# First MLP in eight blocks of 504 positions, the second weight's products interleaved with k's

## The chip, the cores and the metric

The kernel runs on one core of one Trainium2 chip. Its time is the device time of one execution in microseconds; three runs of the kernel before took 1005.41, 1000.34 and 1002.55, median 1002.55. TensorE (PE, with its weight loads PEld), VectorE (DVE), ScalarE (ACT), GpSimd (POOL) and SyncE (SP, which issues the DMAs) run their own instruction lists side by side and wait for each other on semaphores.

## What is computed

Eight batches of 576 positions, 512 features. An attention over 32 memory slots gives x, a first MLP (token shift, squared ReLU, sigmoid gate) gives x2, a second MLP (spatial gate) gives the output:

```python
# attention, per batch and head
a = softmax(phi, axis=positions); k_m = a.T @ k; v_m = a.T @ v
x = softmax(q @ k_m.T / sqrt(64)) @ v_m
# first MLP
x_prev = concatenate([zeros, x[:, :-1]])
xk = mu_k * x + (1 - mu_k) * x_prev
xr = mu_r * x + (1 - mu_r) * x_prev
k = maximum(xk @ w_k, 0.0)                 # 512 -> 1024
v = k * k @ w_v                            # 1024 -> 512
x2 = v / (1.0 + exp(-(xr @ w_r)))          # 512 -> 512
# second MLP
h = maximum(x2 @ w_in, 0.0); u, v = halves(h)
v_s = w_spatial @ layer_norm(v) + b_spatial
out = (u * v_s) @ w_out
```

## The kernel before

Features lie on the partitions, positions in the columns. Every fp32 factor is held as a high and a low part, and a product is three matmuls: high by high, low weight by high, high weight by low (`three`). `split` makes the two parts: a copy on ACT (high, L123) and a subtraction on DVE (low, L124). Weights come in as 64-bit floats, and `load_f64` turns each stretch into fp32 and splits it (ACT L161 and L177, DVE L169, L171 and L178).

The first MLP runs over sixteen half batches of 288 positions (HB). Half batch i has three phases. `k_phase` makes eight products of 12 matmuls (four chunks of features times three) in banks 0 to 3 by turns; each goes through Relu (ACT L725) and, two at a time, Square (L727) and a split into kh and kl (L123, L124). `r_phase` makes four products of 12 matmuls, each with a Sigmoid (L743) into r. `v_product` makes four products of 24 matmuls over the eight chunks of kh and kl, multiplies by r on DVE (L764) and stores x2 to DRAM. That is 240 matmuls of 288 columns. `prep_x` makes the operands xk and xr of the next half batch, 288 columns at a time: two scaled copies of x and x shifted (ACT L432, DVE L436) and a split.

Between the products `pump()` runs the generator `att` one step further, which writes the attention of later batches (`att_step`, two for each batch) into the same instruction lists; its small products use banks 4 to 7. The attention of the first batch (its two steps 0 and 1) is written at the start together with w_k. Step 1 works in borrowed room: its scores lie in the tile `r`, its operands in `kh`, `W3h` and `W3l`. w_v comes in later, into `W3h` and `W3l`, once step 1 is done with them.

Tiles are named by tags with one buffer each: a new tile of a tag waits until the last one has had its last reader. So `tile_of("r", ...)` in `r_phase` waits for step 1 of the attention, and the Relus of the first `k_phase` do not, since they write the tiles `t0` and `t1`. A scheduler orders the list of each engine; PE, ACT and DVE then run their lists in order.

From half batch 13 on, `w_in_steps` brings in and splits w_in. In the last half batch `load_x2(0)` splits the x2 of batch 0 for the second MLP (`uv(0)`), whose first half is written between the last half batch's v products.

Of the kernel before, what the change touches and what calls it, by code (L numbers as in the profile page):

```python
# [27 lines left out]
HALF = 256  # L28
KC = DM // 128
# [17 lines left out]
def kernel(  # L47
# [200 lines left out]
    def att_step(i):  # L248
# [5 lines left out]
        n_small = (3, 0)[i] if i < 2 else 5  # L254
# [77 lines left out]
        for halves in ((0,), (1,)) if i < 2 else ((0, 1),):  # L332
# [3 lines left out]
            scs = {hf: bank(4 + hf)[:, 0:HB] for hf in halves}  # L336
# [48 lines left out]
            if g == 0 and halves[0] == 0:  # L385
                xT[b] = tile_of(f"xT{b % 2}", [128, KC, S + 1])
                nc.gpsimd.memset(xT[b][:, :, 0:1], 0.0)
            for pr in range(2):
# [12 lines left out]
                if i >= 2:  # L401
                    yield True
# [11 lines left out]

    def pump():
        n = slot[0]
        slot[0] += 1
        for _ in range(0 if n < 14 else 3 if n < 28 else 1):
            next(att, None)
        next(more[0], None)  # L420
# [3 lines left out]
    x32_tags = turns("x32a", "x32b")  # L424
    mm = turns(0, 1, 2, 3)

    def prep_x(i, which, c):
        b, hf = divmod(i, 2)
        x32 = tile_of(next(x32_tags), [128, HB])
        n = which * KC + c  # L430

        nc.scalar.activation(  # L432
            out=x32, in_=xT[b][:, c, hf * HB:(hf + 1) * HB], func=ACTF.Copy,
            scale=mu_sb[:, 2 * KC + n:2 * KC + n + 1],
        )
        nc.vector.scalar_tensor_tensor(  # L436
            out=x32, in0=xT[b][:, c, 1 + hf * HB:1 + (hf + 1) * HB], scalar=mu_sb[:, n:n + 1], in1=x32,
            op0=ALU.mult, op1=ALU.add,
        )

        both = operand((n + KC) % (2 * KC) if i == 2 * B - 1 else n)[:, 0:2 * HB]
        h, lo = both[:, 0:HB], both[:, HB:]
        split(x32, h, lo)
        xs[i, which, c] = (h, lo)
# [12 lines left out]
            tile_of("W3h", [128, 4096]), q1, tile_of("r", [128, 2 * S]), tile_of("o0", [128, HB]),  # L457
            tile_of("o1", [128, HB]), tile_of("W3l", [128, n_r], F32R),
# [29 lines left out]
    for c in ORDER:  # L488
# [5 lines left out]
        elif c == "x":  # L494
            prep_x(0, 0, next(xk_chunks))
# [27 lines left out]
    def early(n):  # L523

        for c in FIRST_BLOCK[n]:
            if c == "r":
                next(w_r_steps)
            elif c == "v":
                next(w_v_steps)
            elif c == "n":  # L530
                with tc.issue_after(fetches[-1].ins):
                    load_step(2)
            elif c == "x":
                prep_x(0, 1, next(xr_chunks))
            else:
                stage(first[c == "b"])
# [4 lines left out]
    def w_in_steps():  # L541
# [64 lines left out]
        while not w2_free:  # L606
            yield
        parts_of("W1", wi_u)
        for _ in range(3):
            yield  # L610
        for q, a in ((0, a11), (1, a12), (4, s2), (3, s1), (5, a21), (6, s4), (2, a22)):
            split(a, wi_u[0][:, q], wi_u[1][:, q])
# [3 lines left out]
    last = 2 * B - 1  # L616
    w2_free, xT_free, att_free, late_free, xs_free = [], [], [], [], []
    copied, added, tails, left_v, normal = [None], [None], {}, [], []

    def load_x2(n):  # L620
# [6 lines left out]

        def fetch_x2(dst, k, half):
            sl = slice(half * HALF, (half + 1) * HALF)
            if rest and half == 1:  # L630

                sl = slice(HALF, 2 * HALF - 64)
                for c in range(2):
                    tails[2 * k + c] = dst[:, c, HALF - 64:]
                dst = dst[:, :, 0:HALF - 64]
            src = x2r.rearrange("p c b s -> p c (b s)") if rest else x2d[n]
            nc.sync.dma_start(out=dst, in_=src[:, 2 * k:2 * k + 2, sl])
# [16 lines left out]
        def put(q, x):  # L654
            ts[q] = place(q)

            with behind(*([copied[0]] if rest or (n == 0 and xs_free) else normal if n > 1 else ())):
                split(x, *ts[q])

        if rest:  # L660
# [17 lines left out]
            while not late_free:  # L678
                yield
            yield  # L680
# [4 lines left out]
        else:  # L685
# [14 lines left out]
            while not xs_free:  # L700
                yield
# [11 lines left out]
    def k_phase(i, after=lambda m: None):  # L713
        xk = [xs.pop((i, 0, c)) for c in range(KC)]
        kh, kl = pair("k", [128, FC, HB])
        for m in range(FC):
# [6 lines left out]
            if m % 2 == 0:  # L723
                ks = tile_of(f"t{m // 2 % 2}", [128, 2 * HB])
            nc.scalar.activation(out=ks[:, m % 2 * HB:(m % 2 + 1) * HB], in_=acc, func=ACTF.Relu)  # L725
            if m % 2 == 1:
                nc.scalar.activation(out=ks, in_=ks, func=ACTF.Square)  # L727
                ks = ks.rearrange("p (c s) -> p c s", c=2)
                copied[0] = split(ks, kh[:, m - 1:m + 1, :], kl[:, m - 1:m + 1, :])
            after(m)  # L730
        return kh, kl

    def r_phase(i, after):
        xr = [xs.pop((i, 1, c)) for c in range(KC)]
        r = tile_of("r", [128, KC, HB])
# [9 lines left out]
        return r  # L745

    def v_product(i, m, kh, kl, r, between=lambda: None):
        b, hf = divmod(i, 2)
# [565 lines left out]
```

## Time and profile before

| | |
|---|---|
| median of the runs | 1002.55 us |
| profiled execution | 1001.31 us, of it span 999.5 us |
| PE busy | 976.6 us, 98% of the span |
| DVE, ACT, POOL busy | 704.2, 632.5, 94.7 us |
| mean granted TensorE clock | 0.998 |
| matmuls in the program: 288, 256, 512 columns | 4872, 1596, 336 |

The timeline gives each row's start and length in us; rows of equal instructions are merged, with their number behind x. Busy times of matmuls overlap, so what a matmul costs in a stream is read from the distance between starts. The half batches run from 39 us to some 615 us; w_v is awaited until 79 us; the second MLP takes the rest.

### The profile page before, as it was taken

The page shows a single profiled execution, that of the slowest core. Times are in us where ns is not written, and L with a number is a line of the kernel's source. Part 1 is how long each engine was busy: PE and PEld are TensorE (multiplying, and loading weights), DVE is VectorE, ACT ScalarE, POOL GpSimd, SP SyncE. Part 2 cuts the span into 40 slices and gives each one's busy share as a digit, 9 for nine tenths or more (in the row PEclk, how much of TensorE's full clock was granted, in tenths as well). Part 3 has the DMA queues.
Part 4 walks back from the last instruction along what each step waited for, and adds up shares of the span by engine and source line. Part 5 has one row for each costly group of instructions (what it writes and reads, how often), then busy time and mean ns, then how long its engine had stood idle before and what let it go on. Part 6 is the DMA issues. An engine that isn't in the chain of part 4 may idle for free.

```text
span 999.5 us, 19803 instructions
## 1 busy us (share of the span) xinstructions
PE 976.6 (98%) x7844; PEld 935.6 (94%) x7844; DVE 704.2 (70%) x1477; ACT 632.5 (63%) x1285; POOL 94.7 (9%) x70
## 2 busy tenths in 40 slices
PE   6889999999999999999999999999999999999998
PEld 5778999999999999999999999999999999998787
DVE  4989965665675576567569537768777767779983
ACT  4897884676687667568557647836554644564653
POOL 0000000000000000000013020022012402203320
PEclk9999999999999999999999999999999999999999
DMA  9587422332233323421032142231142223155633
GB/s 285 160 261 243 153 87 68 105 109 98 60 103 115 104 60 93 126 91 31 19 120 82 50 118 68 81 112 37 56 132 90 76 80 90 58 181 168 209 146 116
DMA packets 84300, 110.86 MB, mean 111 GB/s; under 512 B 15984, under 2 KB 67568, under 8 KB 81904
## 3 DMA queue, kind: packets, MB, share of 16 engines
q1 hardware_dynamic: 84208, 109.60, 34.7%
q8 instruction: 61, 1.00, 0.4%
q14 instruction: 31, 0.25, 0.1%
HBM read 79.30 MB, written 30.28 MB: 110 GB/s over the span
## 4 chain that ended last, share of the span: by engine, by line
PE 82%; ACT 6%; DVE 6%; DMA 4%; issue 1%; SPq 0%; POOL 0%; DVEq 0%; ACTq 0%; POOLq 0%
PE bank L104 79%; PE bank L287 2%; DMA st<-in_w_in 2%; DMA st<-in_w_v 1%; DMA ATh<-in_kv 1%; PE bank L339 1%; ACT xT L398 1%; ACT kh L123 1%; DVE xs L124 1%; ACT t L727 1%; ACT t L725 0%; ACT xs L123 0%; ACT x32a L432 0%; DMA st<-in_w_r 0%; ACT st L161 0%
## 5 line engine op out<-in xcount | busy, mean ns | idle before, releaser
L104 PE MATMUL bank<-xs,W1h 128*128 128x288 f32 (+1 forms) x1496 | 246.7, 292 | 2.2 <-DVE o L764 1.2
L104 PEld LDWEIGHTS bank<-xs,W1h 128*128 128x128 f32 x1496 | 211.3, 188 | 7.4 <-issue 5.8
L104 PE MATMUL bank<-xs,W1l 128*128 128x288 f32 (+1 forms) x748 | 135.4, 290 | 0.0
L104 PEld LDWEIGHTS bank<-xs,W1l 128*128 128x128 f32 x748 | 110.6, 188 | 0.2 <-issue 0.2
L104 PE MATMUL bank<-kh,W3h 128*128 128x288 f32 x576 | 98.7, 297 | 2.6 <-ACT W3h L177 2.1
L104 PE MATMUL bank<-xs,W2h 128*128 128x288 f32 (+2 forms) x572 | 97.2, 305 | 1.2 <-ACT xs L123 0.6
L124 DVE TENSOR_TENSOR kl<-t,kh 128x576 fp32r<-128x576 f32 x64 | 49.5, 774 | 59.8 <-ACT kh L123 59.3
L104 PE MATMUL bank<-kh,W3l 128*128 128x288 f32 x544 | 90.0, 296 | 0.0
L104 PEld LDWEIGHTS bank<-xs,W2h 128*128 128x128 f32 x572 | 83.1, 188 | 6.6 <-issue 2.5
L104 PEld LDWEIGHTS bank<-kh,W3h 128*128 128x128 f32 x576 | 83.4, 188 | 5.1 <-ACT W3h L177 3.0
L725 ACT ACTIVATE t<-bank 128x288 f32<-128x288 f32 x128 | 50.9, 402 | 56.9 <-PE bank L104 56.5
L104 PE MATMUL bank<-kl,W3h 128*128 128x288 f32 x544 | 86.1, 296 | 0.0
L104 PEld LDWEIGHTS bank<-kh,W3l 128*128 128x128 f32 x544 | 77.9, 188 | 0.8 <-issue 0.7
L104 PEld LDWEIGHTS bank<-kl,W3h 128*128 128x128 f32 x544 | 77.0, 188 | 0.0
L104 PE MATMUL bank<-ATh,xs 128*128 128x256 f32 x472 | 73.5, 278 | 0.0
L124 DVE TENSOR_TENSOR xs<-st,xs 128x512 fp32r<-128x512 f32 (+1 forms) x60 | 53.4, 904 | 17.2 <-ACT xs L123 17.1
L104 PEld LDWEIGHTS bank<-ATh,xs 128*128 128x128 f32 x472 | 63.2, 188 | 0.0
L123 ACT ACTIVATE xs<-st 128x512 fp32r<-128x512 f32 (+1 forms) x60 | 35.8, 623 | 39.5 <-POOL st L650 35.7
L650 POOL TENSOR_TENSOR st<-st 128x512 f32<-128x512 f32 x16 | 23.5, 1467 | 247.2 <-DVE xs L124 246.5
L104 PE MATMUL bank<-ATl,xs 128*128 128x256 f32 x236 | 46.3, 278 | 0.0
L727 ACT ACTIVATE t<-t 128x576 f32<-128x576 f32 x64 | 43.7, 683 | 1.3
L104 PE MATMUL bank<-xs,W2l 128*128 128x288 f32 x256 | 44.2, 295 | 0.0
(291 smaller groups left out, 2015.2 us busy)
## 6 DMA issues: line engine op xcount, KB each, us to landing
ATh<-in_kv SPq DMA_DIRECT2D x14, 1300.0 KB, 6.6
ATl<-in_qT SPq DMA_DIRECT2D x30, 288.0 KB, 4.4
st<-x2d SPq DMA_DIRECT2D x32, 256.0 KB, 3.9
ATh<-in_phin SPq DMA_DIRECT2D x15, 320.0 KB, 3.1
x2d<-o SPq DMA_DIRECT2D x32, 144.0 KB, 2.0
st<-in_w_in SPq DMA_DIRECT2D x8, 512.0 KB, 4.1
ATh<-gd SPq DMA_DIRECT2D x8, 512.0 KB, 5.2
out_T<-W3h SPq DMA_DIRECT2D x16, 256.0 KB, 2.2
```

What stands on the lines that cost most here:

```text
L104: x = nc.tensor.matmul(out=out, lhsT=pairs[i][0], rhs=pairs[i][1], start=fresh and i == 0, stop=i == n - 1, skip_group_check=not fresh,)
L123: high = nc.scalar.activation(out=h, in_=x, func=ACTF.Copy)
L124: low = nc.vector.tensor_tensor(out=lo, in0=x, in1=h.bitcast(F32), op=ALU.subtract)
L287: x = nc.tensor.matmul(out=kvp[32 * j:32 * j + 32, :], lhsT=ph[0:n, t, 32 * j:32 * j + 32], rhs=kv[0:n, t, j, :], start=(t == 0), stop=(t ...
L339: x = nc.tensor.matmul(out=scs[hf][32 * j:32 * j + 32, :], lhsT=kmT[64 * hf:64 * hf + 64, 32 * j:32 * j + 32], rhs=q[64 * hf:64 * hf + 64, ...
L398: nc.scalar.activation(out=xT[b][:, 2 * g + pr, 1 + hf * HB:1 + (hf + 1) * HB], in_=xo, func=ACTF.Copy)
L650: engine.tensor_tensor(out=out, in0=a, in1=b, op=ALU.subtract)
L725: nc.scalar.activation(out=ks[:, m % 2 * HB:(m % 2 + 1) * HB], in_=acc, func=ACTF.Relu)
L727: nc.scalar.activation(out=ks, in_=ks, func=ACTF.Square)
```

## The change

Half batches 0 and 1 stay as they are in form. The other seven batches (4032 positions) become eight blocks of 504 positions that run across the batches' borders. A block has the same 240 matmuls, with 504 columns each. The order of its products is K0 K1 K2 V0 K3 V1 ... K7 V5 R0 R1 R2 V6 R3 V7: `V(c)` adds the products of chunk c of k to all four v accumulators at once (banks 0 to 3, three matmuls each), so only three chunks of k are kept at a time, in a ring cut from kh and kl (a fourth part holds the last chunk of xr). K and R use banks 4 and 5; the attention keeps banks 6 and 7. `prep_x` works on stretches that end at batch borders and calls the attention on where its x isn't written yet. In `k_phase` the Relus now write into the back of the tile `r`, and r itself is its front. `pump()` runs 0.95 attention steps a call in the blocks. x2 overwrites r and is stored from there. `uv(0)` starts after the last block, v and u mixed, and `load_x2(B)`, which brings the batches' last 64 positions, is called inside it.

```diff
+WB = 504
+NB = (T - S) // WB
...
-        n_small = (3, 0)[i] if i < 2 else 5
+        n_small = (3, 0)[i] if i < 2 else 6
...
-            scs = {hf: bank(4 + hf)[:, 0:HB] for hf in halves}
+            scs = {hf: bank((4 if wide else 6) + hf)[:, 0:HB] for hf in halves}
...
+                while b > 2 and b - 2 not in mixed:
+                    yield True
                 xT[b] = tile_of(f"xT{b % 2}", [128, KC, S + 1])
...
+        while p < p1:
+            b, s0 = divmod(p, S)
+            while b > 0 and G * b + c // G not in written:
+                next(att)
+            w = min(p1 - p, S - s0)
...
-        while not w2_free:
+        while not w1_free:
...
         kh, kl = pair("k", [128, FC, HB])
+        room = tile_of("r", [128, 6, HB])
+        r, ks = room[:, 0:KC], room[:, KC:]
...
-            if m % 2 == 0:
-                ks = tile_of(f"t{m // 2 % 2}", [128, 2 * HB])
-            nc.scalar.activation(out=ks[:, m % 2 * HB:(m % 2 + 1) * HB], in_=acc, func=ACTF.Relu)
+            nc.scalar.activation(out=ks[:, m % 2, :], in_=acc, func=ACTF.Relu)
...
+        x2 = r[:, m, :]
+        nc.vector.tensor_tensor(out=x2, in0=acc, in1=x2, op=ALU.mult)
+        store_x2(m, x2, HB * i, HB * i + HB)
...
-    for i in range(last):
+    for i in range(2):
...
+    pace[:] = 0.0, 0.95
+    rings = [tile_of(tag, [128, 4, WB], F32R) for tag in ("kh", "kl")]
+    slots = [rings[0][:, 0:2], rings[0][:, 2:4], rings[1][:, 0:2]]
+    last_xr = rings[1][:, 2:4].rearrange("p a s -> p (a s)")
+    k_banks = turns(4, 5)
...
+        def K(m):
+            acc = wide_product(wk, m, 0, pump)
+            h, lo = (slots[m % 3][:, n] for n in range(2))
+            x = tile_of("t2", [128, WB])
+            nc.scalar.activation(out=x, in_=acc, func=ACTF.Relu)
+            nc.scalar.activation(out=x, in_=x, func=ACTF.Square)
+            copied[0] = split(x, h, lo)
...
+        def V(c):
+            if c == 0:
+                v_accs.extend(bank(n)[:, 0:WB] for n in range(KC))
+            h, lo = (slots[c % 3][:, n] for n in range(2))
+            for m in range(KC):
+                ms = slice(m * 128, (m + 1) * 128)
+                pairs = (wv[0][:, c, ms], h), (wv[1][:, c, ms], h), (wv[0][:, c, ms], lo)
+                for n, (a, b) in enumerate(pairs):
+                    nc.tensor.matmul(
+                        out=v_accs[m], lhsT=a, rhs=b, start=c == 0 and n == 0,
+                        stop=c == FC - 1 and n == 2,
+                    )
...
+        order = [(K, 0), (K, 1)]
+        for c in range(FC - 2):
+            order += [(K, c + 2), (V, c)]
+        order += [(R, 0), (R, 1), (R, 2), (V, 6), (R, 3), (V, 7)]
+        for n, (f, c) in enumerate(order):
+            f(c)
+            if f is K and c < KC:
+                prep_x(1, c, p0, p1, last_xr if c == KC - 1 else None)
...
+            if n in (13, 14, 15, 16) and j < NB - 1:
+                prep_x(0, n - 13, p1, p1 + WB)
...
+        for m in range(KC):
+            x2 = r_all[0][:, m, :]
+            added[0] = nc.vector.tensor_tensor(out=x2, in0=v_accs[m], in1=x2, op=ALU.mult)
+            store_x2(m, x2, p0, p1)
...
+    for n, item in enumerate(uv(0).items()):
+        item()
+        if n in (2, 12, 14, 16, 18, 23, 25):
+            next(x2_steps)
```

Three places of the instruction lists. ACT in the first half batch, before: t_388 is the Relus' tile, L161 and L177 turn w_r.

```order
L161 ACTIVATE xT_403<-xT_403 128x1024
L432 ACTIVATE x32a<-xT_271,mu 128x288
L725 ACTIVATE t_388<-bank_375 128x288
L432 ACTIVATE x32b<-xT_271,mu 128x288
L725 ACTIVATE t_388<-bank_441 128x288
L727 ACTIVATE t_388<-t_388 128x576
```

ACT now, from the same part of the list on (asp and W3l are the split scores of attention steps 0 and 1, L402 the attention's result, L732 the Relu):

```order
L125 ACTIVATE asp<-ATl 128x288
L163 ACTIVATE xT_576<-xT_576 128x1024
L125 ACTIVATE W3l<-r 128x288
L125 ACTIVATE xs_513<-t_510 128x288
L402 ACTIVATE xT_269<-bank_516 128x288
L402 ACTIVATE xT_269<-bank_521 128x288
L732 ACTIVATE r<-bank_374 128x288
L732 ACTIVATE r<-bank_439 128x288
```

The first two Relus moved behind the split of step 1's scores, which lie in r.

PE in a later half batch, before, where the r products end and the v products begin (rows of the attention between left out):

```order
L104 MATMUL bank_2154<-xs_1898,W2h 128x288
...
L104 MATMUL bank_2185<-kh,W3h 128x288 x8
L104 MATMUL bank_2185<-kh,W3l 128x288 x8
L104 MATMUL bank_2185<-kl,W3h 128x288 x8
L104 MATMUL bank_2229<-kh,W3h 128x288 x8
```

PE now, from the end of K2 through V0 (kh and its neighbour are the ring) to K3:

```order
L106 MATMUL bank_4228<-xs_4063,W1h 128x504
L847 MATMUL bank_4254<-kh,W3h 128x504
L847 MATMUL bank_4254<-kh,W3l 128x504
L847 MATMUL bank_4254<-kh,W3h 128x504
L847 MATMUL bank_4255<-kh,W3h 128x504
...
L847 MATMUL bank_4257<-kh,W3h 128x504
L106 MATMUL bank_4274<-xs_3970,W1h 128x504
```

A v product no longer runs through all chunks in one bank; three matmuls of one chunk go to each of four banks between two products of k.

DVE now, at the border of two blocks (L882 is x2, L454 prep_x, L349 and L358 attention, the last row the low part of K0):

```order
L882 TENSOR_TENSOR r<-bank_3703,r 128x504
L126 TENSOR_TENSOR xs_4225<-t_4220,xs_4225 128x504
L454 SCALAR_TENSOR_TENSOR t_4246<-xT_3196,mu,t_4246 128x360
L454 SCALAR_TENSOR_TENSOR t_4246<-xT_3750,mu,t_4246 128x144
L454 SCALAR_TENSOR_TENSOR t_4297<-xT_3196,mu,t_4297 128x360
L454 SCALAR_TENSOR_TENSOR t_4297<-xT_3750,mu,t_4297 128x144
L126 TENSOR_TENSOR xs_4251<-t_4246,xs_4251 128x504
L349 STREAM_TRANSPOSE ATl<-bank_4182 128x288
L349 STREAM_TRANSPOSE ATl<-bank_4183 128x288
L126 TENSOR_TENSOR kl<-t_4297,kl 128x504
L358 TENSOR_REDUCE ATl<-ATl 128x18
L126 TENSOR_TENSOR kh<-t_4169,kh 128x504
```

Before, x2 was made product by product between prep_x's instructions; now four of 504 columns stand together there, ahead of the low part that V0 reads.

## Rows read from the trace of the kernel before

**Rows 1.** Windows: stretch, length, busy us of each engine (instructions), granted clock, DMA share, GB/s.

```profile
core 0: us, PE busy (x) PEld busy (x) DVE busy (x) ACT busy (x) POOL busy (x), PEclk, DMA share, GB/s
12.00:16.00 4.00, 3.53 (x45) 2.78 (x46) 1.04 (x5) 0.00 (x0) 0.00 (x0) 0.59 1.06 364
...
36.00:60.00 24.00, 21.83 (x156) 20.36 (x156) 23.56 (x50) 22.93 (x50) 0.00 (x0) 1.00 0.53 169
60.00:80.00 20.00, 16.49 (x148) 15.12 (x147) 16.83 (x31) 17.28 (x31) 0.33 (x1) 1.00 0.95 287
...
200.00:480.00 280.00, 279.54 (x2456) 271.14 (x2455) 176.64 (x386) 193.47 (x397) 0.42 (x4) 1.00 0.28 89
600.00:640.00 40.00, 40.00 (x332) 39.87 (x331) 31.44 (x76) 29.54 (x69) 0.00 (x0) 1.00 0.26 80
```

**Rows 2.** Timeline of PE, 288 columns: start, length, engine, line, operands, count.

```profile
317.75 0.69 PE L104 MATMUL bank<-xs,W2l 128*128 128x288 f32 x4
...
322.51 0.69 PE L104 MATMUL bank<-xs,W2l 128*128 128x288 f32 x4
...
323.57 1.22 PE L104 MATMUL bank<-kh,W3h 128*128 128x288 f32 x8
...
329.96 0.70 PE L104 MATMUL bank<-asp 128*128 128x288 f32 x4
```

**Rows 3.** Timeline of PE, 256 columns (second MLP) and 512 columns (last products).

```profile
621.76 0.39 PE L104 MATMUL bank<-xs,W1l 128*128 128x256 f32 x2
...
624.57 0.40 PE L104 MATMUL bank<-xs,W1l 128*128 128x256 f32 x2
...
951.10 0.63 PE L104 MATMUL bank<-W1l,kh 128*128 128x512 f32 x2
...
952.95 1.09 PE L104 MATMUL bank<-W1h,W2l 128*128 128x512 f32 x4
...
955.69 0.62 PE L104 MATMUL bank<-W1h,W2l 128*128 128x512 f32 x2
```

**Rows 4.** Timeline of ACT, PE and DVE in the first half batch.

```profile
42.63 0.41 ACT L725 ACTIVATE t<-bank 128x288 f32<-128x288 f32 x1
...
45.52 1.22 PE L104 MATMUL bank<-xs,W1h 128*128 128x288 f32 x8
...
52.57 0.43 ACT L123 ACTIVATE asp<-ATl 128x288 fp32r<-128x288 f32 x1
...
54.12 0.45 DVE L124 TENSOR_TENSOR W3l<-r,W3l 128x288 fp32r<-128x288 f32 x1
```

**Rows 5.** Groups of ACT, 42.6 to 54.5 us: count, busy us, mean ns, idle before.

```profile
L725 ACT ACTIVATE t<-bank 128x288 f32<-128x288 f32 x6 | 2.3, 394 | 0.3 <-PE bank L104 0.3
L727 ACT ACTIVATE t<-t 128x576 f32<-128x576 f32 x3 | 2.0, 675 | 0.0
L123 ACT ACTIVATE kh<-t 128x576 fp32r<-128x576 f32 x3 | 2.0, 668 | 0.0
```

**Rows 6.** Timeline of PE and ACT while w_v arrives; in brackets idle time and releaser.

```profile
71.34 0.79 PE L104 MATMUL bank<-kh,W3h 128*128 128x288 f32 x4 [1.92 <-ACT W3h L177]
...
82.75 0.43 PE L104 MATMUL bank<-xs,W1h 128*128 128x288 f32 x2
...
78.59 0.67 ACT L177 ACTIVATE W3h<-st 128x512 fp32r<-128x512 f32 x1 [1.12 <-DVE st L171]
```

**Rows 7.** Timeline of PE beside the loading of w_in.

```profile
529.75 0.69 PE L104 MATMUL bank<-xs,W2h 128*128 128x288 f32 x4
530.92 0.80 PE L104 MATMUL bank<-xs,W2h 128*128 128x288 f32 x4 [0.48 <-ACT t L725]
```

**Rows 8.** Groups of DVE, 200 to 480 us.

```profile
L124 DVE TENSOR_TENSOR kl<-t,kh 128x576 fp32r<-128x576 f32 x32 | 24.2, 758 | 34.5 <-ACT kh L123 34.3
L436 DVE SCALAR_TENSOR_TENSOR x32a<-xT,mu,x32a 128x288 f32<-128x288 f32 x32 | 16.4, 513 | 3.0 <-ACT x32a L432 2.7
...
L764 DVE TENSOR_TENSOR o<-bank,r 128x288 f32<-128x288 f32 x31 | 14.0, 452 | 16.7 <-PE bank L104 16.4
...
L347 DVE STREAM_TRANSPOSE ATl<-bank 128x288 f32<-128x288 f32 x16 | 6.9, 461 | 3.3 <-PE bank L339 3.3
```

More of the change, by code (lines that the diff above doesn't have):

```diff
@@ L494 @@
         elif c == "x":
-            prep_x(0, 0, next(xk_chunks))
+            prep_x(0, next(xk_chunks), 0, HB)
         elif c in "ab":
@@ L626, in load_x2 @@
         b11, b12, b21, b22 = raw = [x.rearrange("p (c s) -> p c s", c=2) for x in raw]
+        src = x2r.rearrange("p c b s -> p c (b s)") if rest else x2d[n]
         def fetch_x2(dst, k, half):
[L629 to L637, printed above, removed]
+            nc.sync.dma_start(out=dst, in_=src[:, 2 * k:2 * k + 2, half * HALF:(half + 1) * HALF])
         def place(q):
@@ L655, in put @@
             ts[q] = place(q)
-            with behind(*([copied[0]] if rest or (n == 0 and xs_free) else normal if n > 1 else ())):
+            with behind(*([copied[0], added[0]] if rest or n == 0 else normal if n > 1 else ())):
                 split(x, *ts[q])
@@ L778, in after_r @@
         def after_r(m):
-            prep_x(i + 1, order[0], m)
+            prep_x(0, m, p0, p1)
             if i == 0:
@@ L804, with wide_product @@
-    w2_free.append(True)
-    x2_steps = load_x2(0)
-    next(x2_steps)
-    def after_k(m):
-        next((x2_steps, more[0])[m in (3, 7)], None)
-    kh, kl = k_phase(last, after_k)
-    xs_free.append(True)
+    pace[:] = 0.0, 0.95
[3 more added lines that the diff above has]
+    k_banks = turns(4, 5)
+    def wide_product(w, m, which, between):
+        x = [xs[which, c] for c in range(KC)]
+        acc = bank(next(k_banks))[:, 0:WB]
+        ms = slice(m * 128, (m + 1) * 128)
+        prods = three(
+            [w[0][:, c, ms] for c in range(KC)], [w[1][:, c, ms] for c in range(KC)],
+            [y[0] for y in x], [y[1] for y in x],
+        )
+        gemm(acc, prods, 0, 2)
+        between()
+        gemm(acc, prods, 1, 2)
+        return acc
@@ L819 @@
+    run(more[0])
+    mm = turns(*range(8))
+    for _ in x2_steps:
+        pass
     pieces, ws = [], {}
@@ L985, in items @@
             return [lambda g=groups[k], q=q: g.step(q) for _, k, q in at]
[L987 to L993 removed]
+        return SimpleNamespace(v=v_half, u=u_half, late=late, items=items)
     def store(b, src, c, s0):
@@ L1179 @@
     u_main = tile_of("xT0", [128, KC, 2 * HALF])
-    more[0] = x2_steps
-    next(x2_steps)
-    block.u(lambda at_: late_free.append(True) if at_ == 2 else None)
-    run(more[0])
+    x2_steps = load_x2(B)
+    for n, item in enumerate(uv(0).items()):
+        item()
+        if n in (2, 12, 14, 16, 18, 23, 25):
+            next(x2_steps)
+    for _ in x2_steps:
+        pass
     rest = uv(B)
-    more[0] = chain(block.splits(), w_s_steps([operand(n) for n in (2, 6)], which[:6]))
+    more[0] = w_s_steps([operand(n) for n in (2, 6)], which[:6])
     rest.v()
```

187 lines of the change are left out of this document (92 added, 95 removed).

## The prediction, made before the changed kernel ran

> **What bounds the kernel now.** I read the windows first, the timeline of PE second, then ACT and DVE at the start. In a long stretch of half batches PE is busy 279.54 of 280 us, ACT 193.47 (69%), DVE 176.64 (63%), and the DMA share is 0.28 [rows 1]. So there the time is the number of matmuls by the distance between their starts, and work on ACT, DVE or the queues costs nothing until PE waits for it. At the start it is otherwise: from 36 to 60 us DVE is busy 23.56 and ACT 22.93 of 24, and from 60 to 80 the DMA share is 0.95 with PE busy only 16.49 of 20 [rows 1], since w_v comes in and must be converted; PE stands at 71.34 for a W3h of ACT [rows 6]. So I cost the middle by matmul spacing and the start by who waits for whom. The rest of the second MLP keeps its form.
>
> **1. Wider matmuls.** Removed: 14 x 240 = 3360 matmuls of 288 columns. Added: 8 x 240 = 1920 of 504. The columns are the same, 967,680, so only what a matmul costs beyond its columns can be saved. At 288 columns 36 matmuls of k or r take 317.75 to 322.51, 132.2 ns each, and 48 of v take 323.57 to 329.96, 133.1 [rows 2]; 14 x (144 x 0.1322 + 96 x 0.1331) = 445.4 us, 132.6 ns a matmul. The trace has none of 504. Nearest are those of 512: 951.10 to 955.69 is 20 matmuls, 229.5 ns each (231.3 and 228.3 in its two parts), with 24 of 256 at 117.1 on the other side [rows 3]. The line through 132.6 at 288 and 229.5 at 512 has 0.4326 ns a column; 504 columns cost 226.0 ns, 434.0 us in all: **-11.4 us**. I take this value because 504 is almost 512. Bounds: at 231.3, the dearest 512, 444.1 us, -1.3; at 232.0 (288's price by columns) nothing. Below: 288 columns need 120 ns at 2.4 GHz, the clock granted there (1.00 [rows 1]), so 132.6 holds 12.6 ns beyond them; 504 need 210, and with the same 12.6 are 222.6, 427.4 us, -18.0.
>
> The line through 256 and 512 columns has 4.7 ns a matmul beyond its slope; by it 1440 fewer matmuls give only -6.8, inside the bounds.
>
> The Trainium skill, "TensorE: Matmul & The Clock Gate", section "Back-to-back issue gap", gives N/2.4 + 2.5 ns between isolated matmuls on the fast clock, which speaks against this change: by it 1440 fewer give 3.6 us (an estimate by that page). The rows stand 10 to 14 ns above that formula, and their excess isn't fixed. The section also gives some 131 ns at 512 columns in a stream with weight loads; the trace's 229.5 says no.
>
> **2. The start.** In the first half batch the Relus now write into the tile r, and attention step 1's scores still lie there. Its last reader is DVE's low part, 54.12 + 0.45 = 54.57; the first Relu ran at 42.63 [rows 4]. The order of ACT says the same: it now stands behind the split W3l<-r. One DVE subtraction of 0.758 [rows 8] that stood ahead (kl of the first k chunks) now comes later, so the tile is free some 0.5 us sooner and the first Relu comes around 54.5. PE fills its four banks until 46.05 [rows 4] as before, then has no bank: the fifth k product starts near 54.5 + 0.41 = 55 instead of 46.05, **8.9 us late**. Part of it comes back. Of the 20 us from 60 to 80 PE was idle 3.5, and of the 2.2 idle from 36 to 60 [rows 1] I take 1.0 as lying behind 46; late work fills these. That leaves 8.9 - 4.5 = **+4.4**. The other road: 2.3 + 2.0 + 2.0 = 6.3 us of ACT's work [rows 5] moves behind 54.5, ACT had 20 - 17.28 = 2.7 us free from 60 to 80 [rows 1], so the last w_v conversion, 78.59 [rows 6], slips 3.6 and the v products end at 82.75 + 3.6; the 12 matmuls of the next half batch that had run ahead there [rows 6] are then partly undone, up to 1.6: +3.6 to +5.2. Both roads meet; I keep +4.4. Bounds: +1.6 (conversions on time, only the 12 matmuls lost) to +8.9 (nothing regained).
> The clock: after a shorter pause at the start it was 0.59 from 12 to 16 us [rows 1], between 1.2 and 2.4 GHz. A pause of some 6 us (attention's products break it) may drop it again. Behind the pause PE waits for Relus anyway, so I take 0, and up to +4 for the range.
>
> **3. Stalls beside w_in.** k products of 288 are 12 x 0.132 = 1.6 us apart, and when ACT also converts w_in, PE stands, as at 529.75 to 530.92, waiting for a Relu [rows 7]; 1.17 us between starts four matmuls apart (0.53) leaves 0.64, the largest of three such stalls, 1.35 together by my count. Now a K of 504 and a V stand between, 24 x 0.226 = 5.4 us: **-1.3**; bounds 0 and -1.3.
>
> **4. Borders of blocks.** v accumulators fill banks 0 to 3 for the whole block, so V0 of the next block needs x2 out of them, and also K0's kl. By the order of DVE, four x2, a split, prep_x (two parts of two pieces), another split, transposes and a reduce, and K0's low part stand between V7 and V0. Scaling [rows 8] by columns: x2 452 ns at 288, I take 0.68 at 504, four are 2.7; a low part 0.66 to 0.76, three are 2.1; prep_x's two rows 0.95 each, 1.9; transposes 2 x 0.461; a reduce and the gaps between, an estimate, 1.4. Together 9.0 us. PE runs K0, K1, K2 meanwhile, 36 x 0.226 = 8.1, and DVE's first x2 starts up to 2.0 us ahead of V7's end, as V7's four banks end one after the other 0.68 apart. Slack 8.1 + 2.0 - 9.0 = 1.1. PE should wait little: **+1** in eight borders, bounds 0 and +8 (1 us each, all slack gone).
>
> K and R have two banks instead of four, and attention two for four. A Relu of 504 by [rows 5] is under 0.7 us against 2.7 for a product, so K's banks cost nothing; attention runs between, with ACT and DVE a third free. 0 for both.
>
> **5. After the last block.** uv(0) is no longer mixed with v products; x2's last splits and the layer norms stand on DVE inside its 168 matmuls, 168 x 0.1171 = 19.7 us [rows 3]. DVE was busy 31.44 and ACT 29.54 of 40 there [rows 1], so there are 8.6 us free in twice that time, 4.3 in 19.7. **+1**; bounds 0 and +4. The DMAs carry the same bytes at a share of 0.28 [rows 1]: 0.
>
> **Sum.** -11.4 + 4.4 - 1.3 + 1 + 1 = -6.3. The profiled execution took 1001.31, so 995.0; it stands 1.24 below the median 1002.55, so **996** in runs.
>
> **Rivals.**
> A, cheaper on both ends: 222.6 ns and a start of +1.6. -18.0 + 1.6 - 1.3 + 1 = -16.7: 986. For: an excess per matmul that doesn't grow. Against: it grows from 12.6 to 16.2 between 288 and 512.
> B, the width brings little: 504 at 230 to 232 gives -4 to 0 instead of -11.4; the rest +5.1: 1003 to 1008, say 1005. For: 231.3 was seen, and V alternates four banks and loads a weight for each matmul.
> C, slower: DVE is the bound at each border. If V0's kl comes 3 us later than costed (attention steps ahead of it in DVE's list), 1.1 is slack and 1.9 is lost in each of eight: +15 in place of +1, 1010. It decides from 1.1 us on, and outweighs the gain over all from 1.1 + 7.3 / 8 = 2.0. For: K0's low part stands last of that row on DVE. Against: DVE is 63% busy, and PE has three products ahead.
> D, the change doesn't do what it says: all is as costed, but the start gives nothing back (+8.9): 1000 to 1001.
>
> **How the numbers follow.** Forecast, 0.50: 996, its own range 991 to 1001 from pitch between 224 and 228. A 0.15, B 0.15, C 0.12, D 0.08. A measurement of this kernel can tell some 0.5%, 5 us, from no change: faster is below 997.5, slower above 1007.5. Faster: two thirds of the forecast and A, 0.48. Slower: C and a sixth of B, 0.14. Same: 0.38. Low 986 is A's time; 1008 is B's upper end, and what is left out is C and the far side of A.
>
> **What would show it.** Step 1: the distance between starts of 504-column matmuls in the middle of a block, 226. Step 2: no k product on PE from 46 to 55, the first Relu near 54.5, the last w_v conversion near 82, PE at 1.2 GHz behind the pause or not. Step 3: no wait for Relu near w_in. Step 4: PE's waits at V0 for DVE, none above 1 us. Step 5: a wait of PE for DVE within 20 us behind the last block. A distance of 230 or more, or a wait of 2 us at each border, makes the forecast wrong.

## The result and the profile after

| | before | changed |
|---|---|---|
| median of the runs | 1002.52 us | 1008.98 us (1008.14 to 1010.61) |
| ratio, 95% interval | 1 | 1.0065 (1.0035 to 1.0094); measured again 1.0078 (1.0048 to 1.0108) |
| span of the profiled execution | 999.5 us | 1007.9 us; profiled again 1007.4 us |
| PE busy | 976.6 us | 977.4 us |

The change made the kernel slower by 0.65%, some 6.5 us; 996 was forecast, between 986 and 1008. The windows of the changed kernel answer to [rows 1] (same columns):

```profile
core 0: us, PE busy (x) PEld busy (x) DVE busy (x) ACT busy (x) POOL busy (x), PEclk, DMA share, GB/s
36.00:60.00 24.00, 16.64 (x96) 15.18 (x93) 23.81 (x52) 19.05 (x39) 0.00 (x0) 0.81 0.46 147
60.00:80.00 20.00, 19.19 (x139) 18.70 (x139) 16.27 (x26) 19.15 (x37) 0.11 (x1) 0.98 0.80 232
200.00:480.00 280.00, 278.43 (x1671) 222.32 (x1671) 171.38 (x357) 185.43 (x347) 0.54 (x5) 1.00 0.27 87
600.00:640.00 40.00, 39.72 (x265) 36.39 (x264) 29.82 (x60) 26.65 (x58) 6.22 (x4) 1.00 0.21 64
```

From 36 to 60 us PE lost 5.2 us of work and its granted clock fell to 0.81; in the middle, where it had been busy 279.54 of 280, it is now busy 278.43; and with 1671 matmuls there in place of 2456, little is won. To see where, the two programs are cut at points that stand at the same amount of work: the first products with the keys, the first product behind half batch 1, the first 256-column product of uv(0), the end. PE's timeline of before, then of the changed kernel:

```profile
12.47 0.32 PE L287 MATMUL bank<-ATh 128*32 128x130 f32 x4 [2.79 <-DMA ATh<-in_kv]
123.38 0.29 PE L104 MATMUL bank<-xs,W1h 128*128 128x288 f32 x1
599.90 0.40 PE L104 MATMUL bank<-ATh,xs 128*128 128x256 f32 x2
```

```profile
14.31 0.45 PE L289 MATMUL bank<-ATh 128*32 128x130 f32 x4 [4.78 <-DMA ATh<-in_kv]
131.32 0.39 PE L106 MATMUL bank<-xs,W1h 128*128 128x504 f32 x1
616.03 0.64 PE L106 MATMUL bank<-ATh,xs 128*128 128x256 f32 x4
```

When the keys land varies from run to run: at 14.31 here, between 10.30 and 14.19 in the twelve other profiles of this study. Counted from it, the start takes 117.01 us in place of 110.91, **+6.1**; in the second profile of the changed kernel (12.12 to 129.13) it takes 117.01 again. From there to the 301st 256-column product, from which on only second-MLP work is left (646.33 before, 652.59 after), it is 521.27 in place of 522.95, **-1.7** (second profile 522.93, 0.0; the difference lies in the seventh block and is explained at its pause below). From there to the end 355.33 in place of 353.20, **+2.1** (second profile 355.4), in a part whose form the change left alone.

The matmuls of the last block, which has neither attention nor a pause in it, give the price of 504 columns; its first product and, above, the first 256-column product behind its 240:

```profile
561.29 1.08 PE L106 MATMUL bank<-xs,W1h 128*128 128x504 f32 x4
```

(616.03 - 561.29) / 240 = 228.1 ns, where 226.0 was forecast.

### The profile page after: what moved, and what is told of

It reads as the page before. It is cut to its first block, busy times and chain, and to the rows that moved or that the text cites. A ratio compares the mean times of both kernels' runs of the same rounds, so it can differ in the third digit from the quotient of the medians.

```text
span 1007.9 us, 16735 instructions
## 1 busy us (share of the span) xinstructions
PE 977.4 (97%) x6404; PEld 855.3 (85%) x6404; DVE 692.2 (69%) x1409; ACT 616.8 (61%) x1177; POOL 94.1 (9%) x70
## 4 chain that ended last, share of the span: by engine, by line
PE 73%; DVE 11%; ACT 11%; DMA 3%; issue 1%; POOL 1%; SPq 0%; DVEq 0%; ACTq 0%; POOLq 0%
PE bank L106 58%; PE bank L847 13%; DVE t L454 2%; DVE xs L126 1%; PE bank L289 1%; ACT t L451 1%; DMA st<-in_w_in 1%; DMA ATh<-in_kv 1%; DVE kh L126 1%; DVE r L882 1%; DVE kl L126 1%; ACT t L830 1%; ACT t L829 1%; ACT xs L125 1%; ACT L362 1%
## 5 line engine op out<-in xcount | busy, mean ns | idle before, releaser
L106 PE MATMUL bank<-xs,W1h 128*128 128x504 f32 (+2 forms) x1112 | 240.8, 335 | 0.3 <-ACT xT L943 0.3
L847 PE MATMUL bank<-kh,W3h 128*128 128x504 f32 x384 | 129.1, 393 | 0.0
L106 PE MATMUL bank<-xs,W1l 128*128 128x504 f32 (+2 forms) x556 | 128.3, 335 | 0.0
L106 PE MATMUL bank<-xs,W2h 128*128 128x504 f32 (+3 forms) x316 | 79.8, 371 | 2.9 <-ACT r L837 2.5
L454 DVE SCALAR_TENSOR_TENSOR t<-xT,mu,t 128x288 f32<-128x288 f32 (+6 forms) x128 | 63.0, 512 | 27.1 <-ACT t L451 26.6
L847 PE MATMUL bank<-kh,W3l 128*128 128x504 f32 x192 | 75.1, 391 | 0.0
L829 ACT ACTIVATE t<-bank 128x504 f32<-128x504 f32 x64 | 37.5, 586 | 60.2 <-PE bank L106 52.0
L451 ACT ACTIVATE t<-xT,mu 128x288 f32<-128x288 f32 (+6 forms) x128 | 65.0, 532 | 15.0 <-DVE xs L126 14.3
L126 DVE TENSOR_TENSOR kh<-t,kh 128x504 fp32r<-128x504 f32 x48 | 33.2, 692 | 49.4 <-ACT kh L125 49.2
L126 DVE TENSOR_TENSOR xs<-st,xs 128x512 fp32r<-128x512 f32 (+1 forms) x60 | 52.8, 891 | 13.7 <-ACT xs L125 13.7
L126 DVE TENSOR_TENSOR xs<-t,xs 128x504 fp32r<-128x504 f32 (+1 forms) x72 | 44.4, 624 | 24.3 <-ACT xs L125 24.0
L125 ACT ACTIVATE xs<-t 128x504 fp32r<-128x504 f32 (+1 forms) x72 | 39.6, 577 | 26.4 <-PE bank L106 16.2
```

The costliest lines, as they stand in the source:

```text
L106: x = nc.tensor.matmul(out=out, lhsT=pairs[i][0], rhs=pairs[i][1], start=fresh and i == 0, stop=i == n - 1, skip_group_check=not fresh,)
L125: high = nc.scalar.activation(out=h, in_=x, func=ACTF.Copy)
L126: low = nc.vector.tensor_tensor(out=lo, in0=x, in1=h.bitcast(F32), op=ALU.subtract)
L451: nc.scalar.activation(out=x, in_=xT[b][:, c, s0:s0 + w], func=ACTF.Copy, scale=mu_sb[:, 2 * KC + n:2 * KC + n + 1])
L454: nc.vector.scalar_tensor_tensor(out=x, in0=xT[b][:, c, 1 + s0:1 + s0 + w], scalar=mu_sb[:, n:n + 1], in1=x, op0=ALU.mult, op1=ALU.add,)
L829: nc.scalar.activation(out=x, in_=acc, func=ACTF.Relu)
```

## The experiments

Theory 1 is part 2 of the prediction: the start is lost by the Relus' wait for the tile r. Theory 2: what a matmul costs beyond its columns is set by something else than its width. The rivals stand in each expectation.

### The wait for the scores, alone

`early_relu` undoes it in the changed kernel, `relu_in_r` adds it to the kernel before.

```diff
-            ... tile_of("r", [128, 2 * S]) ...
+    first_room = tile_of("r", [128, 6 * HB])
+            ... first_room[:, 0:2 * S] ...
+        if i == 0:
+            room = first_room.rearrange("p (c s) -> p c s", c=6)
+        else:
+            room = tile_of("r", [128, 6, HB])
```

> The changed kernel with one thing undone: the Relus of the first half batch write into a part of r that attention step 1's scores do not use, so they need not wait for step 1. Theory 1 (the wait costs what the prediction's part 2 said, and stays to the end): the first Relu is back near 43 to 46 us, the gap of some 5 us on TensorE in front of the fifth k product is gone, the clock stays at 2.4 GHz there, the first product of the third stretch (block 0) starts some 4 to 5 us earlier counted from the first k product, and the time falls from 1009.0 by 4 to 5 us to about 1004.5. Rival (the start is bound by the weights of w_v and by ACT's work anyway, so what the Relus win is lost again at w_v): the gap goes, but block 0 starts at most 1 us earlier and the time stays at 1008 to 1009.

```diff
+                if i == 0 and m == 0:
+                    room = tile_of("r", [128, 4 * HB])
+                if i == 0 and m < FC - 2:
+                    ks = room[:, m % 4 * HB:(m % 4 + 2) * HB]
+                else:
+                    ks = tile_of(f"t{m // 2 % 2}", [128, 2 * HB])
```

> The kernel before with only this part of the change added: the Relus of the first three pairs of k chunks of half batch 0 write into the tile r, which step 1's scores hold first. Theory 1: the first Relu near 54 to 57 us, a pause of TensorE of some 5 us, the second half batch late by 4 to 5 us, 1002.5 becomes 1006.5 to 1007.5. Rival (the pause is filled up by work that was waiting for w_v): 1002.5 to 1003.5.

`relu_in_r` came as theory 1 has it: 1.0051 times before (1.0033 to 1.0069), and from the keys (11.99) to the third half batch (127.18) 115.2 us, +4.3. Its timeline has the pause, and the granted clock of 36 to 60 us is 0.86:

```profile
51.24 1.10 PE L104 MATMUL bank<-asp 128*128 128x288 f32 x3 [5.50 <-ACT asp L123]
```

`early_relu` did not: 1.0093 (1.0067 to 1.0119). The pause was gone (first Relu before 47 us), yet block 0 started 117.9 us behind the keys. The time went again in half batch 1; PE's and ACT's timeline there:

```profile
92.78 0.68 PE L106 MATMUL bank<-xs,W1h 128*128 128x288 f32 x4
96.14 0.80 PE L106 MATMUL bank<-xs,W1h 128*128 128x288 f32 x4 [2.67 <-ACT r L736]
```

```profile
95.68 0.71 ACT L736 ACTIVATE r<-bank 128x288 f32<-128x288 f32 x2 [1.28 <-DMA x2d<-r]
```

ACT names what it waits for: a store of x2. In the changed kernel x2 of half batch 0 overwrites r and is stored from there, and the Relus of half batch 1 write a new tile of the same tag, so they wait until the last store has landed. Before, x2 went out of tiles of its own (o0, o1) and the Relus into t0 and t1. It is a second wait on r that I had not seen, and it comes to bear the sooner the first is gone. In the changed kernel it is there too, with the same Relu at 95.30:

```profile
95.30 0.41 ACT L732 ACTIVATE r<-bank 128x288 f32<-128x288 f32 x1 [2.48 <-DMA ATh<-in_phiT]
95.75 1.39 ACT L382 ACTIVATE asp<-ATl 64x576 fp32r<-64x576 f32 x2
```

(The releaser named in this row is another DMA, which landed last by the records. In `rows_512` and `w_out_later`, with the same start, ACT stood 4.15 and 4.60 us there for x2d<-r.) Behind the Relu in ACT's list stands the attention's split, L382, and PE stood 0.75 us, until 97.37, for the part of that split that DVE makes (L383).

### Both waits on r undone

In `own_room` `first_room` serves half batch 1 too, so that only parts that overlap wait for each other. Against `early_relu`:

```diff
-        if i == 0:
-            room = first_room.rearrange("p (c s) -> p c s", c=6)
-        else:
-            room = tile_of("r", [128, 6, HB])
+        room = first_room.rearrange("p (c s) -> p c s", c=6)
```

> The changed kernel with both waits for the tile r at the start undone: half batches 0 and 1 and attention step 1 use one and the same tile, so that only overlapping parts wait for each other. The Relus of half batch 0 then do not wait for step 1's scores, and those of half batch 1 do not wait until the x2 of half batch 0 has been stored from the same tile. Theory 1, mended (two waits in a row on one tile, of which undoing the first alone let the second come to bear: in that run the first Relu of half batch 1 waited until 95.68 us for the store of x2): no pause of TensorE over 1.5 us between 45 and 60 us nor between 88 and 97, from the sixth product matmul of k to block 0 some 84 us as in the kernel before (83.9) instead of 87.5 to 91.6, and the time 4 to 5 us below the changed kernel, about 1.003 times before. Rival (w_v's conversions and the attention bind the start in this layout): 87 us or more to block 0, and the time at 1.006 to 1.009 times before.

1.0037 (1.0015 to 1.0059). From the keys (12.35) to block 0 (123.21) it is 110.86 us, as before (110.91), and the Relu of half batch 1 runs at 86.47:

```profile
123.21 1.07 PE L106 MATMUL bank<-xs,W1h 128*128 128x504 f32 x4
```

```profile
86.47 0.39 ACT L733 ACTIVATE r<-bank 128x288 f32<-128x288 f32 x1
```

One profile doesn't settle this to a tenth. The start took 115.1 to 121.1 us in the six profiles of kernels with both waits, 117.4 on average, and 110.8 to 114.6 in the four with neither, 112.1 on average; the kernel before has one profile. The two groups don't touch, so the two waits are the start's loss in the main. Undoing the first alone won nothing; the second alone was not undone.

From the keys to the end `own_room` takes 989.6 us in place of 993.6, -4.0, and the medians say 3 to 4 as well. So not all of the 6.1 arrives: block 0 takes 63.82 us in place of 63.05, and the 504-column matmuls take 228.5 ns in place of 228.1, 0.8 us in all.

### The pause at 547 us

In the seventh block PE stood 2.53 us ahead of an r product. ACT's timeline of the changed kernel shows where ACT had lost time, 10 us earlier:

```profile
538.88 0.69 ACT L163 ACTIVATE st<-st 128x512 f32<-128x512 f32 x1 [2.11 <-DMA st<-in_w_out]
...
549.59 1.05 ACT L837 ACTIVATE r<-bank 128x504 f32<-128x504 f32 x2
```

The first conversion of w_out stood at the head of ACT's list before its data were there. `w_out_later` fetches each piece two turns ahead and puts the conversion behind the last ACT copy, `behind(copied[0])`; `two_undone` is `own_room` with the conversion behind the last split on both engines:

```diff
-            load_f64(chunks[...], raw=wo_raw[:, :, f0:f0 + 128])
+            piece = fetch(chunks[...])
+            yield
+            yield
+            with behind(*latest):
+                load_f64(piece, raw=wo_raw[:, :, f0:f0 + 128])
```

> The changed kernel, with the four pieces of w_out fetched first and converted two steps later and behind a copy of ACT in the last block, so that no conversion stands at the head of ACT's list before its data are there. Theory: the pause of TensorE at 547 us (2.5 us, r products waiting for a Sigmoid that ACT reaches late) goes, since ACT had idled 2.11 us for that DMA and was behind by as much; the time falls by 2.5 to 2.9 us to about 1006.3. Rival: ACT is behind there from the work of w_in itself (waits for GpSimd and for w_in's DMAs before 538 us), so a pause of 1 to 3 us stays and the time moves by under 1 us.

> The kernel own_room, with the conversions of w_out also kept behind the last split in the program on both ACT and DVE (the earlier try held back ACT's instruction alone; DVE's then stood at the head of its list for the DMA, 1.12 and 1.66 us). Theory: the pause of 2.5 us at the r products of the seventh block goes, and the time is 2.5 to 2.9 us below own_room, about 1.000 times before. Rival (ACT and DVE are late there by the sum of w_in's work): the pause stays above 1 us and the time within 1 us of own_room.

`w_out_later` missed: 1.012 (1.0094 to 1.0146), the pause as long as before. DVE's half of the conversion had not been held back and now stood in front of DVE's list, and the low part behind it (L126) was what ACT then waited 4.10 us for. DVE's timeline:

```profile
542.77 1.02 DVE L171 TENSOR_SCALAR st<-st 128x512 uint32<-128x512 uint32 x1 [1.66 <-DMA st<-in_w_out]
543.71 1.77 DVE L126 TENSOR_TENSOR kh<-t,kh 128x504 fp32r<-128x504 f32 x1
```

In `two_undone` PE's pause at that product is 0.20 us:

```profile
543.88 0.95 PE L106 MATMUL bank<-xs,W2h 128*128 128x504 f32 x3 [0.20 <-ACT r L842]
```

Block 0 to uv(0) takes 483.8 us (126.00 to 609.82) in place of 486.3 in `own_room`, -2.5, all of it in the seventh block (55.31 in place of 57.81; the other seven agree within 0.02). The time is 1.0023 (0.9999 to 1.0046), and its interval overlaps that of `own_room`.

The pause can cost more than its length. Windows of 4 us behind it, in the first profile of the changed kernel and in the second:

```profile
550.00:554.00 4.00, 3.79 (x17) 3.13 (x18) 0.51 (x1) 1.23 (x3) 0.00 (x0) 1.00 0.00 0
```

```profile
548.00:552.00 4.00, 3.76 (x10) 3.08 (x11) 0.54 (x1) 0.67 (x2) 0.00 (x0) 0.57 0.00 0
```

PE had stood 2.53 us in the one and 2.57 in the other. In the first the granted clock stayed at 1.00, in the second it was 0.57 on average, so mostly at 1.2 GHz, and 10 matmuls ran where 17 had. The seventh block took 57.57 and 59.17 us; that is why the second profile is 1.6 us longer in the middle.

### What sets the distance between matmuls

`rows_512` puts each 504-column operand in a row of 512. `pitch` adds series of matmuls behind the last output, with the other engines idle. `moved_64` leaves the changed kernel as it is and only moves tiles in SBUF.

```diff
-        h, lo = both[:, 0:p1 - p0], both[:, p1 - p0:2 * (p1 - p0)]
+        wide = 512 if p1 - p0 == WB else p1 - p0
+        h, lo = both[:, 0:p1 - p0], both[:, wide:wide + p1 - p0]
-    rings = [tile_of(tag, [128, 4, WB], F32R) for tag in ("kh", "kl")]
+    rings = [tile_of(tag, [128, 4, 512], F32R) for tag in ("kh", "kl")]
...
```

> The changed kernel with each 504-column operand (xk, xr, the ring of k) in a row of 512, so that every row begins at a multiple of 64 bytes; the matmuls still have 504 columns. In the changed kernel they start 228 ns apart, 2 more than predicted. Theory A (rows that begin in the middle of a 64-byte line cost the 2 ns): the distance falls to 226 or 227 and the time by 2 to 5 us, to 1004 to 1007. Theory B (the distance belongs to the width; the line through 288 and 512 was off, as the rows of 512 themselves spread from 227 to 236): 228 stays, and the time within 1 us of 1009.

1.0071 (1.0049 to 1.0093): 228.0 ns at 504 columns over some 1800 distances, 228.1 in the changed kernel. Theory A fell: rows that begin off a multiple of 64 bytes cost 0.1 ns in the mean.

```diff
+    def series(width, shift, count=64):
...
+        for n in range(count):
+            at = 1024 + 1024 * (n % 2) + shift
+            nc.tensor.matmul(out=bank(0)[:, 0:width], lhsT=field[:, at:at + 128], rhs=field[:, 0:width], ...)
+    for width in (256, 288, 504, 512):
+        for shift in (0, 16, 32, 48):
+            series(width, shift)
...
```

> The changed kernel with series of matmuls added behind its last output, while all other engines stand still: 64 each of 256, 288, 504 and 512 columns, with the weights' address 0, 64, 128 and 192 bytes beyond a multiple of 256 and the streamed operand's at 0, then 384, 448 and 504 columns. Their distance between starts is what is asked. Theory A (the 228 ns at 504 columns belongs to the width): 504 columns 226 to 229 ns, 512 some 229 to 232, on one line with 288 at 132. Theory B (the work of the other engines or the order of operands makes it): 504 below 225 here. On the second MLP, whose 256-column matmuls got 2 ns slower with addresses as the one difference: if the place of the weights to the streamed operand decides, 256 columns differ by 3 to 5 ns between the four places (cheapest at 64); if not, they agree within 1 ns.

Two starts from the series of 256 columns at 0 bytes (45 matmuls apart) and at 64 (47 apart), then of 504 columns at 0 (48 apart) and at 128 (47 apart):

```profile
1030.03 0.52 PE L1311 MATMUL bank<-ATh 128*128 128x256 f32 x3
1035.43 0.52 PE L1311 MATMUL bank<-ATh 128*128 128x256 f32 x3
1038.13 0.39 PE L1311 MATMUL bank<-ATh 128*128 128x256 f32 x2
1043.46 0.50 PE L1311 MATMUL bank<-ATh 128*128 128x256 f32 x3
1097.74 0.61 PE L1311 MATMUL bank<-ATh 128*128 128x504 f32 x2
1108.62 0.61 PE L1311 MATMUL bank<-ATh 128*128 128x504 f32 x2
1126.66 0.63 PE L1311 MATMUL bank<-ATh 128*128 128x504 f32 x2
1137.62 0.63 PE L1311 MATMUL bank<-ATh 128*128 128x504 f32 x2
```

| weights' address modulo 256 bytes (streamed operand at 0) | 0 | 64 | 128 | 192 |
|---|---|---|---|---|
| 256 columns, ns | 120.0 | 113.3 | 118.7 | 117.8 |
| 288 columns, ns | 131.7 | 133.4 | 133.3 | 132.2 |
| 504 columns, ns | 226.7 | 228.8 | 233.3 | 228.9 |
| 512 columns, ns | 226.7 | 233.3 | 232.4 | 228.9 |

Theory B fell: with nothing else running 504 columns still take 226.7 to 233.3. Theory A holds in part, since no line goes through the widths: at 0 and at 192 bytes 504 columns cost what 512 cost. The weights' address is worth up to 6.7 ns at 256, 504 and 512 columns, and the cheapest address differs with the width. Whether it counts by itself or as the place of the weights to the streamed operand, which the second theory says, the series can't tell, since the streamed operand lies at 0 in all of them.

In the kernel before, ATh lies at 0, the xs tiles but for xs0 at 64 and W1 at 0 (modulo 256, by the tiles' addresses in the program); in the changed kernel, whose tiles shifted, at 0, 128 and 128. So, counted as weights beyond the streamed operand, the 256-column products of the second MLP went from places 64 (xs as weights) and 192 (W1 as weights) to 128 and 0. Their distances, over all 1596, are 116.5 and 118.7 ns. Two rows of each, 12 matmuls apart, before (115.8) and changed (118.3):

```profile
702.01 0.64 PE L104 MATMUL bank<-ATh,xs 128*128 128x256 f32 x4
...
703.40 0.62 PE L104 MATMUL bank<-ATh,xs 128*128 128x256 f32 x4
```

```profile
620.43 0.64 PE L106 MATMUL bank<-ATh,xs 128*128 128x256 f32 x4
...
621.85 0.64 PE L106 MATMUL bank<-ATh,xs 128*128 128x256 f32 x4
```

`moved_64` moves xs to 64 beyond ATh, and W1 to 64 beyond xs:

```diff
-    mask_sb, mu_sb, eps = ...      # ahead of ATl
+    mask_sb, mu_sb, eps = ...      # behind W2
+    for tag, cols in (("st6", 6), ("mv", 2)):
+        nc.vector.memset(tile_of(tag, [128, cols]), 0.0)
```

> The changed kernel with nothing changed but where tiles lie: three small tiles (mask, mu, eps) come behind w_r's tiles and two others ahead of the xs tiles, so that xs begins 64 bytes, modulo 256, beyond ATh and ATl, and W1 64 beyond xs (128 and 0 in the changed kernel). By the added series of the run pitch, 256 columns take 113.3 ns at 64 and 118.7 and 120.0 at 128 and 0; 504 columns take 228.8 at 64 and 226.7 at 0. Theory (the place of the weights to the streamed operand sets what a matmul costs beyond its columns): in the second MLP 256 columns fall from 118.7 to 114 or 115.5 ns, 5 to 7 us over 1596; k's and r's 504 columns rise by up to 2 ns, 0 to 2.3 us over 1152; together 3 to 6 us less than the changed kernel, some 1.001 to 1.004 times before. Rival (256 columns got slower for another reason, such as the order of work around them): 118 to 119 ns stays, and so does the time, 1.006 to 1.009 times before.

256 columns fell to 117.4 ns, and from the 301st of them to the end it is 353.8 us in place of 355.3. Two rows, 12 apart (117.5):

```profile
620.90 0.63 PE L103 MATMUL bank<-ATh,xs 128*128 128x256 f32 x4
...
622.31 0.64 PE L103 MATMUL bank<-ATh,xs 128*128 128x256 f32 x4
```

So addresses alone move the price, in the theory's direction, by under half of its size. Place modulo 256 isn't the whole rule, as the means over the distances of two groups show, beside what the series has for the same place:

| | before | changed | `moved_64` |
|---|---|---|---|
| xs as weights, ATh streamed: place | 64 | 128 | 64 |
| ns in the kernel, in the series | 114.8, 113.3 | 118.6, 118.7 | 117.0, 113.3 |
| W1h as weights, xs streamed: place | 192 | 0 | 64 |
| ns in the kernel, in the series | 117.5, 117.8 | 118.9, 120.0 | 117.6, 113.3 |

The figures are steady: three more profiles with the changed kernel's addresses (`after_again`, `rows_512`, `pitch`) have 118.6 and 118.8 to 118.9. But the same place 64 costs 114.8, 117.0 and 117.6. What in the addresses sets the price stays open, and since no run put the old addresses back, it isn't shown that they make all of the 2.2 ns. The time, 1.0083 (1.0062 to 1.0104), can't tell 1.5 us.

### Together, and the attention's pauses

`two_moved` joins the edits of `two_undone` and `moved_64`.

> The kernel two_undone (no waits for r at the start, w_out converted later) with the tiles moved as in moved_64. If the three costs are separate and add up, it is 3 to 6 us below two_undone: 0.996 to 0.999 times before, which would beat both. Rival (the attention's or ACT's work takes up part of it): 1.000 to 1.003.

0.9988 (0.9966 to 1.0010), 1000.99 against 1001.71: the loss is undone, a gain isn't shown. From the 301st 256-column product to the end it takes 353.8 us in place of 355.4 in `two_undone`, 1.6 less and not 3 to 6. In the changed kernel, by the distances between starts, PE also stood 0.4 to 0.9 us at the attention's last products in most blocks, for DVE's part of the split. `asp_later` gives that split one turn more:

```diff
             yield True
+            if i >= 2:
+                yield False
             if g == 0 and halves[0] == 0:
```

> The kernel two_moved with one turn more between the split of an attention step's scores and the products that read it (one yield in the generator). In each block TensorE stood 0.4 to 0.9 us at those products, waiting for DVE's last part of the split (0.62 us at 269.64 in the changed kernel), which the changed kernel's pace of the attention in the blocks brought about. Theory: these pauses, 3 to 4 us in all, go or halve: 1.5 to 3.5 us below two_moved, 0.995 to 0.998 times before. Rival (the same wait shows up one product later, or prep_x, which needs the attention's result, is late instead): within 1 us of two_moved.

0.9997 (0.9979 to 1.0016). Three of five such pauses in the blocks fell below 0.3 us, but block 0 to uv(0) takes 483.83 us (121.70 to 605.53), `two_moved` 483.98 (126.80 to 610.78). The rival is borne out: what the pauses gave back was lost again elsewhere in the blocks.

Last, the changed kernel once more beside the others, with no edit:

> The changed kernel, unchanged, beside the others on one chip. It was measured in 4 runs so far, 1.0065 times before (1.0035 to 1.0094). Theory (its loss is in the kernel: the two waits for r at the start 4 to 5 us, the w_out pause 2.7, dearer 256 columns 3.5, 504 columns at 228 instead of 226): 1.006 to 1.009 again; the length from the first landing of the first keys to block 0 is 115 to 121 us as in its kin (117.0 in its first profile), against 110.9 before. Rival (a late first landing of data, 14.31 against 12.47 us, made a part of it): under 1.005.

1.0078 (1.0048 to 1.0108), with the keys at 12.12 and again 117.0 us from there to block 0: the loss is the kernel's, and needs no late landing of the keys.

## Why the prediction was wrong

The prediction's sum was -6.3 us, the sum below is +6.6. Of the 12.9 between them 3.9 lie in step 1, 1.7 in step 2 and 2.5 in step 3; 6.8 lie in terms that I had at nothing, the 256-column matmuls (3.5) and the attention in the blocks (3.3). Steps 4 and 5 came out 2 us better than forecast.

**Step 1, wider matmuls: half right.** 228.1 ns at 504 columns make 437.9 us; against 445.4 that is -7.5, not -11.4. The price came from a line through 288 and 512, and 512 from 20 matmuls that took 229.5 [rows 3]. All 331 distances of 512 columns in that trace have a mean of 230.2, and the line through that gives 226.7: the small sample explains 0.7 of the missing 2.1 ns. The rest is the line itself; in the series, too, 504 columns lie on none. Rivals A (a fixed excess) and B (230 and more) both fell; that the time lies just beyond B's upper end is chance and comes from the steps below. By the isolated spacing of the Trainium skill, "TensorE: Matmul & The Clock Gate", section "Back-to-back issue gap", N/2.4 + 2.5 ns, 504 columns would take 212.5 ns, an estimate by that page; no address in the series comes below 226.7. (The 117.1 ns at 256 columns of [rows 3] are 7.9 above that formula, outside the 10 to 14 that I gave for the rows.)

**Step 2, the start: the mechanism right, the size short.** +6.1 for +4.4. The chain foreseen is there: PE stands until asp, then runs the attention's products at the lower clock (0.81 from 36 to 60 us), and the fifth k product starts at 58.78:

```profile
48.96 0.69 PE L106 MATMUL bank<-xs,W1h 128*128 128x288 f32 x4
54.51 1.82 PE L106 MATMUL bank<-asp 128*128 128x288 f32 x6 [4.85 <-ACT asp L125]
57.18 1.81 PE L106 MATMUL bank<-W3l 128*128 128x288 f32 x6 [0.85 <-ACT xT L402]
58.78 1.16 PE L106 MATMUL bank<-xs,W1h 128*128 128x288 f32 x4
```

Six matmuls take some 1.8 us there. Before, at the same place and a clock of 1.00 [rows 1], six of W3l had taken 1.06:

```profile
54.82 1.06 PE L104 MATMUL bank<-W3l 128*128 128x288 f32 x6 [0.18 <-ACT xT L398]
```

I had taken 0 for the clock and not looked at the second reader of r, the store of x2, although the diff says that x2 overwrites r; `early_relu` and `own_room` show that it binds as soon as the first wait is gone. Counted from the keys, the fifth k product comes 10.9 us late (8.9 forecast) and 4.8 of it come back (4.5 forecast). `relu_in_r`, which has the first wait alone, is 9.8 late and gets 5.5 back: that its +4.3 meets the forecast of +4.4 is luck, two errors that cancel. The second road had the last conversion of w_v slip by 3.6 us; it ran at 81.67, which is 1.2 later, counted from the keys, so that road was no second proof.

**Step 3, w_in: the wrong sign.** The three stalls of 1.35 us [rows 7] went, and one of 2.5 us came in the next block, by w_out. I had asked how far the k products stand apart, and not what ACT and DVE wait for at the head of their lists.

**Step 4, borders: 0 for +1.** DVE at a border of two blocks, and PE's first V0 product there:

```profile
254.28 2.44 DVE L882 TENSOR_TENSOR r<-bank,r 128x504 f32<-128x504 f32 x4
...
261.44 0.67 DVE L126 TENSOR_TENSOR kh<-t,kh 128x504 fp32r<-128x504 f32 x1
```

```profile
264.41 0.39 PE L847 MATMUL bank<-kh,W3h 128*128 128x504 f32 x1
```

K0's low part (in kh) is done at 262.11, 2.3 us ahead of V0: the slack was 2.3 and not 1.1. DVE took 7.8 us from the first x2 and not 9.0, and K0 to K2, with attention's products among them, 9.05 and not 8.1; against that, the first x2 started 1.1 us ahead of V7's end and not 2.0. No V product of the eight blocks waited, so rival C fell with it.

**Step 5, behind the last block:** one wait of 0.44 us, by the distance between starts, for +1. What I had at nothing is the form that the change doesn't touch: 1596 matmuls of 256 columns became 2.2 ns dearer, 3.5 us, while their tiles shifted; `moved_64` shows that addresses alone change this price, not that they make all of it. No step of mine could have found it, as none asked where tiles lie.

**The sum again,** from the keys on, for the first profile: -7.5 for the width, +6.1 for the start, +3.5 for 256 columns, and in the blocks all that is not a product of the first MLP (attention's products and pauses) 46.8 us in place of 42.3, +4.5: +6.6, against +6.55 measured (8.39 less 1.84 of landing). The 46.8 are 131.32 to 616.03 less the 437.9; the 42.3 are 123.38 to the last v product's end at 620.83, less the 445.4 and 84 products of 256 columns, 9.8 us. Of the 4.5, 1.2 is w_out's pause less the three stalls. The other 3.3 stay open: the attention's pauses are the visible part, but the one run that halved them got nothing back.

## What to carry to other kernels

When a tile takes over the room of others, list every reader of the old tiles with the time at which it ends, stores to DRAM among them; two waits in a row on one tile can hide each other, and undoing the first alone may then show nothing, as here. A saving per matmul of a few per cent is of the size of what a matmul gains or loses by where its operands lie, so take its price from many rows, and count the matmuls whose addresses merely shift.

## What the runs showed of the hardware

The distance between matmuls depended on the addresses of their operands: 113.3 to 120.0 ns at 256 columns and 226.7 to 233.3 at 504, as the weights' address went through 0, 64, 128 and 192 modulo 256 bytes, with all other engines idle and the clock at 1.00. In the kernels, moving tiles alone took 256-column matmuls from 118.7 to 117.4 ns. The distance did not depend on whether DVE and ACT were busy beside the matmuls: a fit over the 1805 distances of 504 columns in the changed kernel puts their influence at under 1 ns.

Behind a pause of TensorE of some 2.5 us the granted clock stayed at 1.00 in one execution of the changed kernel and was 0.57 over the next 4 us in another; that block took 1.6 us longer there.
